# A long convolution and a feed-forward net in one kernel: the first unit's entry rearranged, and a new written-out order

## The chip, the cores and the metric

The kernel runs on one core of a Trainium2 chip. A time is the device time of one execution in microseconds (us). The kernel before took 345.71 us (median of four runs, 345.22 to 345.76). A profile holds one execution, from the core's first instruction to its last; that stretch is its span. The engines of the core work side by side, each through its own queue in order: TensorE (PE, with its weight loads PEld), VectorE (DVE), ScalarE (ACT), GpSimd (POOL), and SyncE (SP), which issues most DMA transfers. They wait for each other by semaphores. Matmul results lie in PSUM and have to be read from there (evicted) by DVE or ACT before the space is used again.

## The reference

Two layers; each adds a gated long convolution and then a feed-forward net to x, which is 2048 rows of 512 columns in bfloat16.

```python
def conv(q, k, v, shift_k, ssm_k, ssm_D):        # all [S=2048, D=512]
    k_shift = sum(pad(k)[t:t + S] * shift_k[:, 3 - t] for t in range(4))
    kv = k_shift * v
    y = irfft(rfft(kv, 2 * S) * rfft(ssm_k.T, 2 * S))[:S]   # causal, per column
    return q * (y + kv * ssm_D)

def ffn(x):                                      # w_gate, w_up: 512 x 1792; w_down: 1792 x 512
    return (silu(x @ w_gate) * (x @ w_up)) @ w_down

for layer in range(2):
    x = x + conv(layernorm(x), k, v, shift_k, ssm_k, ssm_D)
    x = x + ffn(layernorm(x))
```

y does not depend on x, so it is worked out once and used in both layers.

## The kernel before

**Tiling.** The 2048 rows are four blocks of 512. Inside a block row 4p+r lies on partition p as residue r, so a block is a tile of 128 partitions by four rows (r = 0 to 3) by 512 columns. A unit of the feed-forward net is (layer, block, half), two residues, 256 rows. The net (`ffn`) runs over 14 strips of 128 hidden columns: gate and up products of two strips go to a PSUM tile `pf` of 128x512, ACT applies silu to the gate tile (L965) and copies the up tile (L969), DVE multiplies them (L972), and `wd_sb` matmuls (L985) add up in two PSUM tiles `pd`, one for each row. The tile `zT` holds the normalised input with columns on partitions.

**Convolution.** A block's k is turned so that columns lie on partitions, four shifted copies are multiplied by diagonal matrices `dg` of the taps on TensorE, and the sum is multiplied with v on DVE (`shift_mul`, L523 for block 0, L513 and L514 for block 1). Fourier sums by table matmuls (`fwd`) give spectra X of kv and G of the filter, in four slots of a real and an imaginary part. `half` makes G's parts `ev`, which DVE adds and subtracts (`butterfly`, L444 and L446). `product` multiplies X and G on DVE slot by slot (L641, L645) into Z. `inverse_half` forms sums and differences m of Z (L790) and turns them back with table `inv` (L796) into four PSUM tiles, one for each residue; `evacuate_y` (L716) copies tiles to Y on ACT. Later blocks follow while the net runs.

**Entry of the first unit.** `prologue` with `on_pe` multiplies the normalised rows n by y, row 0 straight from PSUM (L902), row 1 from Y (L905), adds them to x (L907), takes the mean and variance (`ln_stats`, L808 to L811, and the power -1/2 on POOL, L813) for both rows together, normalises (L863), turns on TensorE (L919) and copies to `zT` (DVE L922, ACT L924). Other units turn z by DMA (L892). While the entry waits, TensorE works on block 1: its filter's transform, its `shift_mul` and its X.

**Order.** Nothing is left to a scheduler. `Plan.add` records every operation with its engine, an assumed cost, and the buffers that it reads and writes; `Plan.order` takes one list, ORDER, that gives each operation its rank, and lays it in that sequence on its engine's queue. The same walk gives each tile its place in a small ring of buffers: four PSUM tiles `pf`, two `pc`, two `pd`. Costs and `due` times steer the search that made the list and the choice of the ring's place; they execute nothing. In the gaps that the costs foresee before 32 us, `issue` puts filler matmuls (`wm`).

**Around the start.** SP loads h, k, v and x of block 0 and then the weights. Block 0's k is loaded with rows on partitions, turned by TensorE (L365) into PSUM, and copied to `kTb` by `transpose_k` with the four residues interleaved again, two tiles on ACT (L371) and two on DVE (L373). ACT takes the statistics of x's first rows (L827 to L837).

Of the kernel before, what the change touches and what calls it, by code (L numbers as in the profile page):

```python
# [36 lines left out]
KTE = "ADAD"  # L37
# [5 lines left out]
H_SPLIT = False  # L43
PWA = 2.4
# [6 lines left out]
ORDER = [0, 5, 63, 1, 9, 7, 2, 10, 3, 6, 4, 8, 12, 16, 13, 11, 14, 15, 17, 19, 18, 24, 20, 22, 25, 29, 30, 41, 21, 26, 31, 38, 45, 35, 43, 32, 55,  # L51
         42, 51, 64, 74, 59, 71, 100, 104, 70, 76, 23, 27, 28, 37, 53, 39, 65, 44, 36, 34, 50, 58, 69, 72, 47, 40, 33, 46, 56, 62, 48, 61, 49, 60,
         57, 66, 54, 67, 52, 88, 116, 150, 236, 155, 73, 84, 85, 89, 93, 79, 80, 82, 83, 86, 75, 77, 91, 94, 98, 90, 96, 97, 99, 102, 87, 81, 92,
         101, 95, 106, 110, 144, 170, 165, 185, 109, 113, 105, 107, 112, 111, 114, 118, 103, 108, 68, 78, 115, 120, 119, 123, 139, 130, 121, 124,
         127, 125, 129, 132, 140, 142, 148, 134, 138, 141, 154, 158, 161, 136, 146, 152, 117, 122, 128, 126, 133, 137, 143, 145, 160, 147, 173, 178,
         168, 163, 177, 174, 151, 156, 131, 135, 176, 180, 162, 189, 164, 183, 169, 175, 205, 211, 149, 172, 218, 222, 190, 202, 153, 157, 159, 166,
         179, 195, 167, 171, 188, 197, 182, 184, 186, 187, 192, 194, 207, 225, 199, 209, 198, 248, 216, 191, 204, 196, 203, 206, 200, 208, 210, 214,
         215, 219, 226, 230, 237, 224, 228, 233, 231, 241, 246, 256, 249, 258, 262, 275, 274, 280, 277, 283, 287, 291, 296, 292, 298, 299, 302, 309,
         313, 318, 319, 323, 245, 239, 252, 261, 255, 257, 271, 265, 201, 213, 221, 212, 223, 229, 181, 193, 217, 220, 227, 250, 326, 329, 294, 301,
         285, 289, 235, 244, 238, 284, 312, 324, 264, 268, 293, 305, 332, 339, 345, 347, 354, 350, 330, 232, 242, 438, 300, 279, 310, 320, 328, 336,  # L60
         358, 367, 388, 400, 418, 408, 424, 433, 452, 448, 459, 470, 463, 467, 466, 471, 486, 491, 530, 534, 472, 483, 535, 529, 561, 600, 612, 638,
         234, 240, 251, 263, 259, 270, 243, 260, 254, 267, 276, 304, 286, 247, 253, 266, 272, 278, 282, 281, 303, 306, 321, 317, 273, 311, 297, 308,
         290, 295, 269, 288, 315, 327, 333, 314, 322, 307, 316, 325, 331, 335, 334, 338, 343, 359, 352, 361, 340, 351, 337, 344, 362, 368, 370, 348,
         357, 360, 371, 363, 380, 374, 383, 394, 406, 402, 356, 376, 378, 391, 389, 401, 382, 395, 405, 411, 414, 393, 407, 398, 410, 415, 422, 420,
         426, 423, 429, 341, 346, 342, 349, 353, 364, 365, 366, 369, 372, 375, 379, 384, 381, 385, 387, 390, 396, 399, 403, 404, 409, 444, 458, 441,
         456, 462, 464, 474, 476, 478, 484, 489, 497, 492, 499, 503, 505, 517, 526, 514, 518, 436, 447, 446, 451, 428, 445, 425, 430, 481, 510, 494,
         450, 477, 455, 469, 460, 473, 475, 490, 500, 522, 516, 480, 501, 442, 457, 468, 487, 434, 439, 506, 533, 528, 502, 509, 488, 520, 524, 537,
         539, 546, 544, 551, 685, 580, 386, 419, 435, 461, 449, 482, 485, 511, 504, 519, 531, 555, 559, 542, 554, 560, 563, 571, 574, 581, 585, 437,
         496, 397, 413, 498, 513, 540, 527, 545, 548, 578, 589, 590, 593, 604, 607, 631, 667, 616, 618, 377, 373, 412, 355, 432, 421, 443, 427, 532,
         550, 562, 565, 493, 495, 508, 523, 521, 525, 541, 553, 453, 465, 507, 512, 572, 567, 610, 597, 583, 605, 632, 622, 536, 479, 440, 392, 538,  # L70
         591, 602, 599, 629, 623, 416, 595, 431, 454, 515, 614, 626, 635, 640, 658, 662, 651, 645, 690, 694, 720, 723, 697, 703, 727, 730, 698, 701,
         708, 719, 706, 716, 734, 741, 733, 736, 752, 747, 771, 767, 762, 764, 692, 417, 696, 816, 650, 643, 655, 670, 665, 684, 688, 715, 781, 777,
         788, 792, 814, 800, 822, 830, 837, 861, 866, 869, 874, 880, 875, 879, 894, 896, 876, 882, 889, 892, 888, 893, 904, 937, 923, 942, 954, 948,
         961, 966, 973, 984, 1000, 1037, 557, 569, 547, 556, 573, 579, 564, 568, 586, 596, 624, 587, 598, 603, 611, 592, 606, 577, 584, 619, 634,
         639, 543, 549, 570, 575, 552, 558, 566, 576, 594, 637, 659, 601, 609, 582, 588, 617, 646, 666, 649, 669, 677, 680, 683, 630, 647, 648, 654,
         656, 661, 636, 642, 664, 672, 678, 641, 657, 627, 633, 613, 625, 608, 644, 660, 681, 686, 663, 673, 620, 628, 653, 671, 615, 621, 676, 687,
         691, 674, 679, 668, 675, 682, 689, 695, 693, 699, 702, 704, 709, 710, 721, 722, 732, 700, 712, 742, 770, 761, 735, 753, 729, 738, 749, 756,
         717, 726, 759, 786, 779, 744, 750, 754, 768, 740, 748, 758, 763, 773, 790, 783, 774, 780, 766, 784, 787, 793, 796, 797, 801, 804, 705, 711,
         707, 713, 714, 718, 725, 724, 728, 731, 739, 745, 737, 746, 751, 755, 760, 765, 769, 772, 776, 807, 812, 810, 813, 820, 823, 829, 835, 832,
         842, 844, 848, 852, 850, 854, 856, 858, 865, 870, 878, 868, 872, 839, 845, 819, 825, 824, 831, 799, 827, 815, 821, 834, 860, 863, 828, 838,  # L80
         805, 811, 847, 851, 836, 853, 859, 867, 871, 802, 806, 809, 817, 855, 864, 833, 840, 873, 881, 886, 849, 862, 841, 846, 877, 895, 890, 907,
         917, 1054, 946, 743, 778, 782, 789, 785, 791, 795, 826, 883, 900, 908, 915, 918, 911, 919, 922, 925, 936, 938, 941, 940, 950, 885, 891, 898,
         920, 929, 930, 965, 976, 972, 981, 988, 994, 999, 1001, 1003, 1009, 1018, 1021, 1034, 1045, 1036, 1040, 757, 652, 794, 775, 803, 808, 798,
         818, 843, 857, 979, 986, 978, 982, 910, 914, 901, 913, 897, 905, 884, 887, 947, 951, 991, 996, 1004, 1010, 1013, 1007, 1029, 1015, 997,
         1041, 963, 1025, 983, 955, 1061, 969, 1055, 1069, 927, 1052, 1066, 1035, 1022, 1064, 1068, 1085, 1093, 1113, 1098, 1105, 1118, 1142, 1144,
         1148, 1153, 1147, 1151, 1181, 1185, 1168, 1172, 1155, 1158, 1170, 1173, 1174, 1179, 1160, 1162, 1188, 1195, 1199, 1204, 1208, 1202, 1110,
         1058, 1046, 1063, 1107, 1073, 1124, 1145, 1166, 1212, 1215, 1232, 1239, 1247, 1242, 1251, 1255, 1259, 1264, 1268, 1284, 1271, 1274, 1277,
         1281, 1279, 1283, 1293, 1304, 1291, 1299, 899, 903, 902, 909, 924, 931, 906, 921, 934, 944, 949, 935, 945, 928, 933, 939, 952, 912, 926,
         958, 971, 989, 956, 962, 916, 943, 932, 959, 953, 957, 970, 992, 1002, 964, 974, 960, 967, 977, 1024, 1006, 1032, 1031, 1043, 1056, 1050,
         975, 1020, 980, 990, 1012, 1017, 968, 987, 1023, 1042, 1038, 1008, 1014, 998, 1005, 985, 993, 995, 1011, 1027, 1057, 1051, 1026, 1049, 1033,  # L90
         1047, 1019, 1039, 1030, 1044, 1053, 1060, 1065, 1048, 1059, 1016, 1028, 1062, 1070, 1067, 1074, 1072, 1076, 1080, 1089, 1082, 1087, 1077,
         1083, 1075, 1078, 1071, 1088, 1097, 1108, 1129, 1115, 1122, 1112, 1116, 1095, 1126, 1091, 1096, 1128, 1139, 1136, 1086, 1099, 1119, 1132,
         1103, 1109, 1127, 1130, 1135, 1143, 1150, 1133, 1137, 1100, 1106, 1141, 1146, 1154, 1149, 1157, 1079, 1084, 1081, 1090, 1092, 1094, 1102,
         1101, 1104, 1111, 1114, 1120, 1117, 1121, 1123, 1125, 1131, 1134, 1138, 1140, 1152, 1163, 1159, 1164, 1165, 1169, 1178, 1175, 1180, 1184,
         1189, 1193, 1196, 1203, 1197, 1206, 1209, 1219, 1223, 1226, 1229, 1177, 1186, 1156, 1167, 1161, 1176, 1171, 1182, 1192, 1201, 1205, 1211,
         1214, 1194, 1207, 1213, 1218, 1190, 1200, 1222, 1235, 1230, 1198, 1224, 1217, 1221, 1183, 1210, 1187, 1191, 1228, 1238, 1244, 1225, 1234,
# [14 lines left out]
R = 4  # L111
# [126 lines left out]
def kernel(  # L238
# [117 lines left out]
    def transpose_k(b, ring, engs):  # L356
# [3 lines left out]
        for dt in range(KD):  # L360
            pt = new("pc" if dt < 2 else "pd", "pt", [P, R, P], BF16)

            def go(pt=pt, dt=dt):
                for r in range(R):
                    nc.tensor.transpose(pt.t[:, r, :], kn[b].t[:, r, dt * P:(dt + 1) * P], ident.t[:])  # L365
# [921 lines left out]
```

## Time and profile before

| what | us |
|---|---|
| median of four runs | 345.71 |
| the profiled execution's own time | 345.45 |
| its span | 343.7 |
| h of block 0 lands, its turn on TensorE starts | 4.37, 4.41 |
| products X by G start on DVE (L641) | 15.06 |
| second sum m on DVE (L790) | 25.21 |
| row 0 times y (L902) | 26.66 |
| both rows normalised (L863) | 31.38 to 32.12 |
| first feed-forward matmul | 33.46 |

A profile line of a timeline gives start, length, engine, source line, operation, the tile written and those read, shapes, and how many; in brackets stands how long the engine was idle in front of it and what ended that. The lines of a table by stretch give the busy time of each engine with its count of instructions, then TensorE's granted clock as a share (1.00 throughout), the DMA engines' share, and GB/s. Instructions of one engine overlap, so what an instruction costs its engine is the distance between two starts, not its length.

### The profile page before, as it was taken

The page shows a single profiled execution, that of the slowest core. Times are in us where ns is not written, and L with a number is a line of the kernel's source. Part 1 is how long each engine was busy: PE and PEld are TensorE (multiplying, and loading weights), DVE is VectorE, ACT ScalarE, POOL GpSimd, SP SyncE. Part 2 cuts the span into 40 slices and gives each one's busy share as a digit, 9 for nine tenths or more (in the row PEclk, how much of TensorE's full clock was granted, in tenths as well). Part 3 has the DMA queues.
Part 4 walks back from the last instruction along what each step waited for, and adds up shares of the span by engine and source line. Part 5 has one row for each costly group of instructions (what it writes and reads, how often), then busy time and mean ns, then how long its engine had stood idle before and what let it go on. Part 6 is the DMA issues. An engine that isn't in the chain of part 4 may idle for free.

```text
span 343.7 us, 6604 instructions
## 1 busy us (share of the span) xinstructions
PE 338.5 (98%) x2616; PEld 248.1 (72%) x2616; DVE 279.6 (81%) x479; ACT 253.8 (74%) x503; POOL 40.7 (12%) x46
## 2 busy tenths in 40 slices
PE   8999999999999999999999999999999999999996
PEld 6656868777588757778587767767686877777683
DVE  8799999999999997999999999979998524535112
ACT  7899988989788538977699997569774635546362
POOL 4100111102113001212020001111101000100000
PEclk9999999999999999999999999999999999999999
DMA  7999111091110144132101020610202120101101
GB/s 285 312 293 323 43 31 63 15 159 41 34 46 17 31 97 120 23 63 70 32 7 41 2 76 2 127 28 1 32 0 50 26 37 0 24 8 27 41 13 31
DMA packets 42089, 22.96 MB, mean 67 GB/s; under 512 B 33861, under 2 KB 39882, under 8 KB 42058
## 3 DMA queue, kind: packets, MB, share of 16 engines
q1 hardware_dynamic: 41904, 22.47, 26.6%
q8 instruction: 20, 0.33, 0.4%
q14 instruction: 11, 0.09, 0.1%
q10 hardware_dynamic: 154, 0.07, 0.1%
HBM read 12.33 MB, written 2.10 MB: 42 GB/s over the span
## 4 chain that ended last, share of the span: by engine, by line
PE 92%; DVE 3%; DMA 2%; ACT 1%; SPq 0%; issue 0%; ACTq 0%
PE pf L310 57%; PE pd L985 28%; PE ps L310 5%; DMA xc<-in_A_q_dram 2%; DVE t L641 1%; DVE Z L645 1%; PE ps L796 1%; DVE m L790 1%; PE pd L944 1%; ACT jk L833 0%; ACT jk L827 0%; DVE G L444 0%; PE ptz L919 0%; DVE G L446 0%; ACT ev L418 0%
## 5 line engine op out<-in xcount | busy, mean ns | idle before, releaser
L310 PE MATMUL pf<-zT,wg_sb 128*128 128x256 bf16 x896 | 111.0, 273 | 0.0
L310 PE MATMUL pf<-zT,wu_sb 128*128 128x256 bf16 x896 | 110.9, 273 | 0.0
L985 PE MATMUL pd<-wd_sb,ht 128*128 128x512 bf16 (+1 forms) x462 | 105.5, 373 | 0.0
L310 PEld LDWEIGHTS <-wu_sb 128*128 128x128 bf16 x896 | 87.7, 98 | 17.4
L310 PEld LDWEIGHTS <-wg_sb 128*128 128x128 bf16 x896 | 87.7, 98 | 16.3 <-issue 0.3
L965 ACT ACTIVATE sg<-pf 128x512 bf16<-128x512 f32 x112 | 65.4, 604 | 24.4 <-PE pf L310 20.2
L969 ACT CAST ht<-pf 128x512 bf16<-128x512 f32 x112 | 65.0, 594 | 23.5 <-PE pf L310 19.8
L985 PEld LDWEIGHTS <-ht 128*128 128x128 bf16 x462 | 45.2, 98 | 42.8
L972 DVE TENSOR_TENSOR ht<-ht,sg 128x1024 bf16<-128x1024 bf16 (+1 forms) x64 | 39.2, 619 | 24.3 <-ACT ht L969 17.3
L813 POOL TENSOR_TENSOR rstd<-ve,nhalf 128x2 f32<-128x2 f32 x24 | 29.4, 1228 | 204.8 <-DVE ve L811 204.8
L808 DVE BATCH_NORM_STATS2 bnst<-xc 128x6 f32<-128x512 bf16 x48 | 31.5, 685 | 1.9 <-ACT xc L1011 1.3
L1021 ACT CAST dn<-pd 128x512 bf16<-128x512 f32 x24 | 13.5, 594 | 21.5 <-PE pd L985 21.5
L1024 DVE TENSOR_TENSOR xc<-xc,dn 128x1024 bf16<-128x1024 bf16 x12 | 8.3, 689 | 18.7 <-ACT dn L1021 18.5
L652 DVE TENSOR_TENSOR t<-X,G 128x2048 bf16<-128x2048 bf16 x18 | 21.9, 1217 | 0.1
L656 DVE TENSOR_TENSOR t<-X,G 128x2048 bf16<-128x2048 bf16 x18 | 21.9, 1217 | 0.0
L418 ACT ACTIVATE X<-ps 128x512 bf16<-128x512 f32 x32 | 18.9, 611 | 1.0 <-PE ps L457 0.5
L839 POOL TENSOR_TENSOR rstd<-ve,nhalf 128x2 f32<-128x2 f32 x8 | 7.7, 958 | 65.1 <-ACT ve L837 65.1
L418 ACT ACTIVATE H<-ps 128x512 bf16<-128x512 f32 x24 | 13.9, 607 | 1.7 <-PE ps L310 1.5
L664 DVE TENSOR_TENSOR t<-t,t 128x2048 bf16<-128x2048 bf16 x12 | 14.7, 1221 | 0.1
L666 DVE TENSOR_TENSOR Z<-Z,t 128x2048 bf16<-128x2048 bf16 x12 | 14.6, 1220 | 0.1
L310 PE MATMUL ps<-hs,fwd 128*128 128x512 bf16 x40 | 12.5, 379 | 0.3 <-ACT H L418 0.3
L603 ACT ACTIVATE kc<-kTb,tapF 128x512 bf16<-128x512 bf16 x16 | 12.4, 802 | 0.0
(109 smaller groups left out, 325.4 us busy)
## 6 DMA issues: line engine op xcount, KB each, us to landing
hn<-in_A_ssm_k_dram SPq DMA_DIRECT2D x4, 512.0 KB, 6.2
vt<-in_A_v_dram SPq DMA_DIRECT2D x4, 512.0 KB, 6.7
xc<-in_A_q_dram SPq DMA_DIRECT2D x4, 512.0 KB, 4.1
out_dram<-xc SPq DMA_DIRECT2D x15, 128.0 KB, 1.8
wg_sb<-in_B_w_gate_dram SPq DMA_DIRECT2D x1, 1792.0 KB
wu_sb<-in_B_w_up_dram SPq DMA_DIRECT2D x1, 1792.0 KB, 8.2
wd_sb<-in_B_w_down_dram SPq DMA_DIRECT2D x1, 1280.0 KB, 11.5
kn<-in_A_k_dram SPq DMA_DIRECT2D x1, 512.0 KB, 4.4
```

Source lines behind the costliest of these rows:

```text
L310: nc.tensor.matmul(o, lhsT=lhsT, rhs=rhs, start=(n == 0), stop=(n == len(terms) - 1))
L418: add("ACT", act(D), lambda: nc.scalar.activation(out=view(), in_=ps.t[:], func=ACT.Copy, scale=scale), r=[ps], w=[(buf, keys)], conv=conv)
L652: dve(n * D, lambda t1=t1, part=part: nc.vector.tensor_mul(out=t1.t[:], in0=x.t[:, sl, 0, :], in1=g.t[:, sl, part, :]), [(x, key(slots, (0 ...
L656: dve(n * D, lambda t2=t2, part=part: nc.vector.tensor_mul(out=t2.t[:], in0=x.t[:, sl, 1, :], in1=g.t[:, sl, 1 - part, :]), [(x, key(slots ...
L664: dve(n * D, lambda t1=t1, t2=t2, comb=comb: nc.vector.tensor_tensor(out=t1.t[:], in0=t1.t[:], in1=t2.t[:], op=comb), [t2], [t1], conv=conv)
L666: dve(n * D, lambda t1=t1, part=part: nc.vector.tensor_add(out=z.t[:, sl, part, :], in0=z.t[:, sl, part, :], in1=t1.t[:]), [t1], [zk], con ...
L808: add("DVE", 0.6, lambda st=st, i=i: nc.vector.bn_stats(out=st.t[:], in_=xs[c].t[:, i, :]), r=[(xs[c], (i,))], w=[st])
L813: add("POOL", pw, lambda: nc.gpsimd.tensor_tensor(out=rstd.t[:], in0=ve.t[:], in1=nhalf.t[:].to_broadcast((P, n)), op=ALU.pow), r=[ve, nha ...
L965: add("ACT", act(D), lambda ps=ps, o=o, sg=sg: nc.scalar.activation(out=sg.t[:, o:o + 2, :], in_=ps.t[:], func=ACT.Silu), r=[ps], w=[(sg, ...
L969: add("ACT", act(D), lambda ps=ps, o=o, ht=ht: nc.scalar.copy(out=ht.t[:, o:o + 2, :], in_=ps.t[:]), r=[ps], w=[(ht, (o // 2,))], due=(uni ...
L972: dve(n * W, lambda sg=sg, ht=ht: nc.vector.tensor_mul(out=ht.t[:], in0=ht.t[:], in1=sg.t[:]), [sg], [ht], due=(unit, k / pairs, 0.0, "h"))
L985: nc.tensor.matmul((pds[o] if not cs.start else pds[HP]).t[:, cs], lhsT=ht.t[:, q, o * P:(o + 1) * P], rhs=wt["d"].t[:, ft, cs], start=(ft ...
```

## The change

- **Turned k.** `kTb` of block 0 becomes [128, 4 column tiles, 4 residues, 129] with a zero in front of each residue. The four copies out of PSUM are dense, and all on DVE. `shift_mul` reads shifted rows as another residue, dense.
- **Row 1 of the first unit from PSUM.** YD = 2: rows 0 and 1 are multiplied from PSUM; their evictions to Y stay and come after the product.
- **Row by row.** PST: each of the two rows has its own variance and power. FS = 4: of the first two strip pairs, the gate and up tiles are made in two halves of 128 columns, one for each row, so that the first half reads row 0 of `zT` alone.
- **Orders.** ORDER is a new list, of 1577 operations in place of 1571. Read off the two lists, what differs most near the start: the ACT evictions of `ev` parts a and c all come before the statistics of x; one of the G sums (L446) is put before the products with v; ACT's `ve` (L837) comes after the evictions of X's first slot; one product L641 more stands before the first m, and the difference m of the first pair (L790) comes after the second pair's sum; two of block 1's four `shift_mul` rows come before the second pair's inverse; one product L652 for block 1 comes before the second half-unit's L885, not after. SP loads x of block 1 before the second part of `wd_sb`. POOL makes `fq` before the identity. After that the lists hold the same work in other interleavings.
- **Constants.** Assumed costs are changed, and branches are added that the flags leave unused (K_SPLIT, VE_DVE, H1E, "mix", "tapsk").

```diff
-KTE = "ADAD"
+KTE = 'DDDD'
+FS = 4
+PST = True
+YD = 2
...
-        kT[b] = new("k", "kTb", [P, KD, PADL + L], parts=KD + 1)
-        add("POOL", 0.2, lambda: nc.gpsimd.memset(kT[b].t[:, :, 0:PADL], 0.0), w=[(kT[b], (KD,))], due=-48)
+        kT[b] = new("k", "kTb", [P, KD, R, P + 1], parts=KD + 1)
+        add("POOL", 0.2, lambda: nc.gpsimd.memset(kT[b].t[:, :, :, 0:1], 0.0), w=[(kT[b], (KD,))], due=-48)
...
-            dst = lambda dt=dt: kT[b].t[:, dt, PADL:PADL + L].rearrange("d (p r) -> d p r", r=R)
-            src = lambda pt=pt: pt.t[:].rearrange("d r p -> d p r")
+            dst = lambda dt=dt: kT[b].t[:, dt, :, 1:P + 1]
+            src = lambda pt=pt: pt.t[:]
...
+            def at(dt, s):
+                if b:
+                    return kT[b].t[:, dt, PADL + s:PADL + s + R * (P - 1) + 1:R]
+                return kT[b].t[:, dt, s % R, 1 + s // R:1 + s // R + P]
...
-        evacuate_y(k, range(1, R))
+        evacuate_y(k, range(YD, R))
...
-            if i == 0:
-                ps = fresh[c][0]
+            if i in range(YD):
+                ps = fresh[c][i]
...
-                evacuate_y(c, (0,))
+                evacuate_y(c, (i,))
...
-        st = ln_stats(c, rows, 0.85)
+        sts = [ln_stats(c, [i], 0.85) for i in rows] if PST else [ln_stats(c, rows, 0.85)] * HP
...
-            zop = normalise(z, (0,), lambda z=z: z.t[:], c, i, o, st)
+            zop = normalise(z, (0,), lambda z=z: z.t[:], c, i, 0 if PST else o, sts[o])
...
+                    split = unit == (0, 0, 0) and 2 * k + (which == "u") < FS
...
+                    def part(ps=ps, o=o, which=which, fts=fts, i=0):
+                        for q in (0, 1):
+                            ft = fts[o + q]
+                            mm(ps.t[:, q * W + i * P:q * W + (i + 1) * P],
+                               [(wt[which].t[:, kd, ft * P:(ft + 1) * P], zT.t[:, kd, i]) for kd in range(KD)])
...
+                    if split:
+                        for i in range(HP):
+                            add("PE", pe(2 * KD, P), lambda part=part, i=i: part(i=i), r=[(zT, (i,)), wt[which]], w=[(ps, (i,))], due=due)
+                    else:
+                        add("PE", pe(2 * KD, W), go, r=[zT, wt[which]], w=[ps], due=due)
```

## The prediction

> **What bounds the kernel now.** I read the page's first part, then busy time by stage, then TensorE's timeline where the stages show gaps, then VectorE's over the same time. The first lines are the page's busy times and its chain.
>
> ```profile
> PE 338.5 (98%) x2616; PEld 248.1 (72%) x2616; DVE 279.6 (81%) x479; ACT 253.8 (74%) x503; POOL 40.7 (12%) x46
> PE 92%; DVE 3%; DMA 2%; ACT 1%; SPq 0%; issue 0%; ACTq 0%
> ```
>
> TensorE is 92% of the chain. Busy time by stretch (us; length, then PE, PEld, DVE, ACT, POOL, then clock and DMA) says where it is not full:
>
> ```profile
> 4.40:22.00 17.60, 17.41 (x162) 11.25 (x163) 15.74 (x36) 16.01 (x36) 3.63 (x7) 1.00 1.12 302
> 22.00:26.00 4.00, 3.25 (x28) 1.91 (x27) 3.97 (x10) 4.00 (x9) 0.00 (x0) 1.00 1.01 392
> 33.46:46.00 12.54, 12.54 (x106) 10.36 (x106) 12.31 (x19) 11.89 (x29) 1.71 (x2) 1.00 0.19 37
> 46.00:100.00 54.00, 54.00 (x403) 39.15 (x400) 52.71 (x88) 48.28 (x100) 8.14 (x8) 1.00 0.27 55
> 100.00:200.00 100.00, 100.00 (x756) 73.77 (x754) 95.32 (x144) 78.46 (x151) 13.19 (x9) 1.00 0.20 47
> ```
>
> From 33.46 us, where the first feed-forward matmul starts, TensorE has no gap: the end lies a fixed amount of TensorE work behind that point. Only idle time before it can be won, and only by TensorE doing something else in it. TensorE's timeline (start, length, line, shape, count):
>
> ```profile
> 23.10 0.38 PE L796 MATMUL ps<-m,inv 128*128 128x512 bf16 x1
> 23.32 0.28 PE L1253 MATMUL wm<-wz 128*128 128x128 bf16 x2
> 23.89 0.38 PE L310 MATMUL ps<-hs,fwd 128*128 128x512 bf16 x1 [0.30 <-ACT H L418]
> 24.38 0.38 PE L796 MATMUL ps<-m,inv 128*128 128x512 bf16 x1
> 24.59 1.05 PE L310 MATMUL ps<-dg,kTb 128*128 128x128 bf16 x16
> 25.96 0.81 PE L796 MATMUL ps<-m,inv 128*128 128x512 bf16 x3 [0.31 <-DVE m L790]
> 26.61 0.38 PE L310 MATMUL ps<-hs,fwd 128*128 128x512 bf16 x1
> 26.82 1.24 PE L796 MATMUL ps<-m,inv 128*128 128x512 bf16 x5
> 27.90 1.06 PE L310 MATMUL ps<-dg,kTb 128*128 128x128 bf16 x16
> 28.80 0.38 PE L310 MATMUL ps<-hs,fwd 128*128 128x512 bf16 x1
> ```
>
> Matmuls overlap, so pace is read from starts: 5 of width 512 take 26.82 to 27.90, 0.216 each; 16 of width 128 take 27.90 to 28.80, 0.056 each. Idle is a distance between starts less that pace. 24.59 to 25.96 is 1.37 for 0.90 of work: 0.47 idle. 23.89 to 24.38: 0.27. 23.32 to 23.89 holds two fillers only: 0.57. 21.62 to 22.02 in the same view: 0.18. Sum 1.49. The same subtraction where the first unit begins (31.45 to 31.85, the eight transposes from 31.85 to 32.41, 33.06 to 33.46) gives 0.19 + 0.11 + 0.18 = 0.48. So 1.97 us can be won here. Before 22 us TensorE's one other gap (0.34, kn's DMA, before 5.68) stays: the loads keep their order. VectorE is what TensorE waits for at 25.96:
>
> ```profile
> 23.76 1.42 DVE L645 TENSOR_TENSOR Z<-t,t 128x512 bf16<-128x512 bf16 x4
> 25.21 1.29 DVE L790 TENSOR_TENSOR m<-Z 128x1024 bf16<-128x1024 bf16 x2
> 26.66 0.69 DVE L902 TENSOR_TENSOR n<-n,ps 128x512 bf16<-128x512 bf16 x1 [0.15 <-ACT H L418]
> ```
>
> **The change part by part.** VectorE's instructions overlap too; its paces from starts are 0.602 (128x1024 pairs, L641, L790), 0.335 (128x512, L645, L514, L922), 0.67 (a product with a float32 PSUM operand, L523, 10.07 to 10.74 to 11.41).
>
> *Turned k.* Two strided copies on ACT (L371, 0.47 apart) and two on DVE (L373, 0.60 apart: 7.45 to 8.05) become four dense ones on DVE. The nearest dense row is L922, PSUM to SBUF, 0.335: DVE 4 x 0.335 - 2 x 0.60 = +0.14, ACT -0.94. Both lie under TensorE, which is unbroken from 5.68 to 22.0 and gets the same matmuls in another order: nothing by itself. The new copies start at an odd element of rows of 129, which no row here shows; the bounds are 0.335 and the strided 0.60. I take 0.335, since the step is 1 as in L922. At 0.60 DVE carries 1.06 more and the four vt products (L523) end about 0.75 later.
>
> [...]
>
> *Spectrum of block 0.* ACT, relieved, evicts the fourth ev part before the statistics of x (before: 13.25), so one of the two G sums (L446, 0.60) fits in front of the vt products, where DVE sat idle 0.75 (before 10.07), and the other after them. But the product run (L641, 15.06) waits for X0's evictions, not for G. These gain only what ACT puts behind them, the tiny ve (L837, 0.19): start 14.85, 0.21 earlier; bounds 0 and 0.5 (ACT also loses one eviction in front, 0.48).
>
> *The run to the inverse.* From 15.06 to the second sum m at 25.21 is 10.15. The new order takes one difference (L790, 0.602) out of it, behind that sum: 14.85 + 9.55 = 24.40. TensorE, walked along its new order with the paces above: end of block 1's second turn 21.45, first m ready 21.8 (idle 0.3; one product more now lies before it); six spectrum and inverse matmuls (1.30) with 0.1 for the late hs eviction; then two 16-matmul convolutions, moved up from 24.6 and 27.9, fill to 25.0. Their kTb landed at 21.63. Second sum ready 25.15 (idle 0.15), two matmuls, the moved difference 25.75 (idle 0.15). Idle in all 0.7 against 1.49: **-0.79**.
>
> *Row 1 from PSUM, row by row.* The product L902 moves from 26.66 to 26.2. Row 1's product (L905, 0.41) becomes a PSUM one: +0.335 on DVE. In return it waits for two matmuls, not for ACT's eviction (0.60) behind them; that eviction stays, later, on ACT. Row 0 gets its own ve (0.09) and rstd (POOL, two columns took 0.80; POOL idle 15.4 before it). Walk from 26.2: 0.72 product, 0.46 sum, 0.67, 0.61, 0.33, 0.12 aggregate, 0.19 ve, POOL 0.80 from 29.2 to 30.0; DVE meanwhile row 1's statistics and one vt product, to 30.5; z row 0 to 30.9 (before, both rows 31.38 to 32.12). TensorE arrives at 30.7 (31.67 for the same set, less the 0.79 and one matmul moved behind): idle 0.3 instead of 0.48, as row 0's transposes, the two residual adds and row 1's transposes now hide the rest: **-0.18**. Queued behind the added DVE work is conv block 1 (L539 and on), up to 0.4 later.
>
> *Split matmuls.* Four tiles as 16 of width 128 instead of 8 of width 256 (0.108, 40 in 4.37): 4 x (0.90 - 0.87) = **+0.13**.
>
> *Evictions at the start of the unit.* ACT gains nothing there; it is full from 22 to 44.5, and TensorE comes 0.8 to 1 earlier. The fifth to seventh gate and up tiles need PSUM freed by L965 and L969, with two squares (L833, 0.85 each with the accumulator read) interleaved. Bounds 0 and 0.35 on the third; I take 0, the trace having 40 us of those two lines waiting for TensorE and none the other way.
>
> *SP, POOL, costs.* x of block 1 is loaded before the second part of wd (landing 34.34, first used after 46) and so 512 KB earlier, 1.5 us at 347 GB/s: no user nears it. POOL's iota before the identity keeps m4 at 1.6. Cost constants and unused flags run nothing.
>
> Sum: -0.79 - 0.18 + 0.13 = -0.84, from the profiled execution's own 345.45 (span 343.7, 1.75 lies around it and is untouched) to 344.6; from the median 345.71, 0.26 higher, to **344.9**. A kernel like this, whose runs spread over 0.54, can hardly be told from unchanged within 0.2% (0.69 us): 345.02 to 346.40.
>
> **Rivals.**
> - *More than the walk*: all 1.97 goes, less the 0.13: 343.9. For: my walk keeps each wait at its worst. Against: DVE is 99% busy in 22 to 26 (3.97 of 4.00).
> - *Second half-unit late.* In before its second zT transpose is issued at 49.60 and lands 2.4 later, 52.0, against its first use at 53.02: 1.0 of slack. VectorE is full (12.31 of 12.54), carries 0.4 more, and one 1.14 product (L652) now stands in front of L885, its chain: -0.46 + 0.42 + 1.14 = 1.1 later less small gaps, say 0.7. TensorE wants it 0.8 earlier: wait 0.5. Time 345.4. Against: L652 then isn't behind it.
> - *The odd start halves the copies.* vt 0.75 late, of which TensorE's queue hides about half: product run 0.4 later, 345.3.
> - *Slower: an eviction is late in the long part.* The new order of some 1,500 operations must keep 100% from 33 to 340 us. Each time a PSUM tile is freed one ACT instruction late costs its pace, 0.48; two such use up the gain, four give 344.9 + 1.9 = 346.8. For: ACT 48.28 of 54 and DVE 95.32 of 100. Against: no such wait in before.
> - *No effect at all* can't be: four copies change engine and shape.
>
> **How the numbers follow.** Forecast 0.45 (its own range 344.4 to 345.2: the walk's waits put 0.3 to 0.5 either way), more 0.15, half-unit late 0.14, odd start 0.08, late evictions 0.18. Faster (under 345.02): all of the second, four fifths of the forecast, a tenth of the two middle cases: 0.15 + 0.36 + 0.02 = 0.53. Slower (over 346.40): most of the last, 0.16. Same: the rest, 0.31. The range runs from 343.9, the bound of what can be won, to 346.4, where two to three late evictions would put it and about half of the last case is left out.
>
> **What would show it.** Right: the four kTb copies near 0.41 long on DVE; the second m sum near 24.4; TensorE's idle between 21 and 26 near 0.7; the first feed-forward matmul at about 32.2, on 128 columns; no gap after 35. Wrong: kTb copies of 0.68; a TensorE wait for L965 or L969, or at about 52 for zT; X0's evictions not earlier than 15.4.

## The result, and the profile after

The changed kernel takes 346.07 us (median of 45 executions), the kernel before 345.66 (median of 64 beside it): 0.41 us more, a ratio of 1.0016 with a 95% interval of 1.0009 to 1.0022. The forecast was 344.9. The time lies inside the range given and on the other side of no change. Three executions of the experiments below (one of after_fourth, two of after_ht) took 351 us at a lower granted clock (0.993 to 0.995) and are left out of the medians.

The profiled execution of the changed kernel took 347.11 us, its span is 344.5. The page's first part and its chain:

```profile
PE 339.5 (99%) x2646; PEld 249.2 (72%) x2646; DVE 278.6 (81%) x482; ACT 252.8 (73%) x501; POOL 44.0 (13%) x47
PE 92%; DVE 5%; POOL 1%; issue 1%; ACT 0%; POOLq 0%
```

TensorE is as large a part of the chain as before, DVE a larger one. Busy time by stretch (length, then PE, PEld, DVE, ACT, POOL, clock and DMA), with the third stretch again from the first feed-forward matmul, now at 32.88:

```profile
22.00:26.00 4.00, 3.73 (x44) 2.62 (x42) 3.97 (x9) 3.97 (x10) 0.00 (x0) 1.00 0.99 372
32.88:46.00 13.12, 13.12 (x144) 11.32 (x143) 13.02 (x19) 13.09 (x33) 1.57 (x1) 1.00 0.56 127
46.00:100.00 54.00, 53.94 (x399) 38.76 (x398) 51.94 (x88) 48.89 (x100) 9.78 (x8) 1.00 0.17 36
100.00:200.00 100.00, 99.91 (x752) 73.29 (x751) 96.41 (x147) 78.40 (x152) 15.85 (x9) 1.00 0.22 48
```

Between 22 and 26 TensorE is busy 3.73 us instead of 3.25, so the head did what it was to do. But the two last stretches, which were exactly full, have gaps: 53.94 of 54.00 and 99.91 of 100.00.

TensorE's timeline of a second profile of the same kernel (label after_again below), lines that answer to those of before:

```profile
22.00 0.38 PE L819 MATMUL ps<-m,inv 128*128 128x512 bf16 x1 [0.25 <-DVE m L813]
22.21 0.59 PE L317 MATMUL ps<-hs,fwd 128*128 128x512 bf16 x2
22.64 0.38 PE L819 MATMUL ps<-m,inv 128*128 128x512 bf16 x1
23.04 0.59 PE L317 MATMUL ps<-hs,fwd 128*128 128x512 bf16 x2
23.47 1.95 PE L317 MATMUL ps<-dg,kTb 128*128 128x128 bf16 x32
25.26 0.90 PE L819 MATMUL ps<-m,inv 128*128 128x512 bf16 x3
...
32.22 0.39 PE L317 MATMUL ps<-vt,fwd 128*128 128x512 bf16 x1
32.45 1.06 PE L317 MATMUL pf<-zT,wg_sb 128*128 128x128 bf16 x16
```

Two convolutions (32 matmuls, x32) stand where TensorE idled before. Distances between starts less the pace give 0.41 before 22.00, 0.18 before 23.04 and 0.09 inside the three matmuls from 25.26: 0.69 us of idle, against 1.49 before. VectorE at the same place, in the same profile:

```profile
24.43 1.90 DVE L813 TENSOR_TENSOR m<-Z 128x1024 bf16<-128x1024 bf16 x3
26.24 0.68 DVE L929 TENSOR_TENSOR n<-n,ps 128x512 bf16<-128x512 bf16 x1
```

The second sum starts at 24.43 and row 0's product at 26.24, where before had 25.21 and 26.66.

**Where the time went back.** Each profile is cut in three at two marks that both kernels have: the start of the first feed-forward matmul, and the last matmul of all. The clock column is from the clock records of the trace: until that moment matmuls of 128 columns start 0.107 us apart, from then on 0.056. (The clock share of 1.00 in the tables by stretch holds only from there on.)

| kernel, profile | full clock from | first feed-forward matmul | from there to the start of the last matmul | from its end to the end of the span | span |
|---|---|---|---|---|---|
| before | 4.04 | 33.46 | 306.92 | 3.03 | 343.7 |
| before, again | 6.74 | 33.88 | 306.92 | 3.03 | 344.1 |
| changed, the profile above | 6.42 | 32.88 | 307.88 | 3.44 | 344.5 |
| changed, after_again | 4.35 | 32.45 | 307.67 | 3.49 | 343.9 |
| changed, after_third | 4.66 | 32.52 | 307.67 | 3.48 | 343.9 |
| changed, after_fourth | 7.38 | 33.33 | 307.68 | 3.34 | 344.6 |

The first unit begins 1.0 us earlier, and that is lost again in two places: 0.75 in the long part and 0.3 to 0.46 behind the last matmul. (Some 0.4 of the 0.75 is not loss: matmuls that came before the first mark and now follow it, worked out below.) The chip's own contribution, the moment of the full clock, moves either kernel by as much as the whole result: between an early and a late one lie 0.42 us at the first feed-forward matmul of before and 0.88 at that of the changed kernel.

### The profile page after: what moved, and what is told of

It reads as the page before. It is cut to its first block, busy times and chain, and to the rows that moved or that the text cites. A ratio compares the mean times of both kernels' runs of the same rounds, so it can differ in the third digit from the quotient of the medians.

```text
span 344.5 us, 6659 instructions
## 1 busy us (share of the span) xinstructions
PE 339.5 (99%) x2646; PEld 249.2 (72%) x2646; DVE 278.6 (81%) x482; ACT 252.8 (73%) x501; POOL 44.0 (13%) x47
## 4 chain that ended last, share of the span: by engine, by line
PE 92%; DVE 5%; POOL 1%; issue 1%; ACT 0%; POOLq 0%
PE pf L317 53%; PE pd L1024 28%; PE ps L317 7%; POOL rstd L836 1%; PE ps L819 1%; DVE t L664 1%; PE wm L1305 1%; DVE bnst L831 1%; PE pt L494 1%; DVE ht L1011 1%; PE ps L475 1%; PE pd L971 1%; DVE Z L668 0%; DVE m L562 0%; PE pt L379 0%
## 5 line engine op out<-in xcount | busy, mean ns | idle before, releaser
L317 PE MATMUL pf<-zT,wg_sb 128*128 128x256 bf16 (+1 forms) x912 | 110.8, 271 | 0.1
L317 PE MATMUL pf<-zT,wu_sb 128*128 128x256 bf16 (+1 forms) x912 | 109.9, 271 | 0.0
L1008 ACT CAST ht<-pf 128x512 bf16<-128x512 f32 x112 | 63.9, 595 | 21.1 <-PE pf L317 19.3
L836 POOL TENSOR_TENSOR rstd<-ve,nhalf 128x2 f32<-128x2 f32 (+1 forms) x25 | 28.1, 1123 | 206.3 <-DVE ve L834 195.7
L866 POOL TENSOR_TENSOR rstd<-ve,nhalf 128x2 f32<-128x2 f32 x8 | 12.4, 1550 | 61.5 <-ACT ve L864 61.5
L626 ACT ACTIVATE ka<-kTb,tapF 128x512 bf16<-128x512 bf16 x16 | 12.4, 792 | 0.0
```

Source lines behind the costliest of these rows:

```text
L317: nc.tensor.matmul(o, lhsT=lhsT, rhs=rhs, start=(n == 0), stop=(n == len(terms) - 1))
L836: add("POOL", pw, lambda: nc.gpsimd.tensor_tensor(out=rstd.t[:], in0=ve.t[:], in1=nhalf.t[:].to_broadcast((P, n)), op=ALU.pow), r=[ve, nha ...
L1008: add("ACT", act(D), lambda ps=ps, o=o, ht=ht: nc.scalar.copy(out=ht.t[:, o:o + 2, :], in_=ps.t[:]), r=[ps], w=[(ht, (o // 2,))], due=(uni ...
```

## Experiments

Medians are of 9 to 12 executions of each kernel, beside 29 to 34 of the kernel before on the same chip. The same changed kernel lies 0.27, 0.98 and 0.98 above before in three jobs (sets of runs side by side), the same changed head 0.43 below and 0.02 above it: the differences scatter by up to 0.7 us, more than some effects asked for. Only for order_head, head_nosplit, after_third, after_fourth, after_ht and after_ht_act7 does the 95% interval of the ratio to before leave out 1. The profile's own marks are sharper, and verdicts below rest on them where medians don't decide.

| kernel | median us | before, same job | difference |
|---|---|---|---|
| after_again | 346.00 | 345.73 | +0.27 |
| head_after | 345.30 | 345.73 | -0.43 |
| tail_after | 346.46 | 345.73 | +0.73 |
| after_act7 | 345.61 | 345.38 | +0.23 |
| head_act3 | 345.70 | 345.38 | +0.32 |
| order_head | 347.50 | 345.38 | +2.12 |
| head_nosplit | 346.47 | 345.38 | +1.09 |
| after_third | 346.54 | 345.56 | +0.98 |
| after_act7_second | 345.56 | 345.56 | 0.00 |
| head_again | 345.58 | 345.56 | +0.02 |
| head_act7 | 345.44 | 345.56 | -0.12 |
| after_fourth | 346.41 | 345.43 | +0.98 |
| after_ht | 345.96 | 345.43 | +0.53 |
| after_ht_act7 | 346.06 | 345.43 | +0.63 |

The span of every execution is on record too. Pooled over the jobs of the experiments and the result, the medians are 343.8 us for before (124 executions), 344.2 for the changed kernel (79), 343.45 for the changed head (24, head_after and head_again), and 343.7 for the changed kernel with seven copies on ACT (24, after_act7 and after_act7_second).

### Head or long part: the order cut in two

Two kernels take the order apart at its 420th operation, about where the first unit begins. `head_after` has the changed operations:

```diff
-ORDER = [the changed sequence]
+ORDER = [its first 420 operations, then all others in the sequence of before]
```

`tail_after` has the operations of before, their first 420 in the sequence of before and the rest in the changed one. With them went the two kernels themselves.

> The changed kernel once more, to see how much of the profiled execution is its own. Clock theory: the first transposes at 0.107 us a matmul until 6.4 us are a state of TensorE's clock that differs from run to run; in another execution the 0.056 pace can begin near 4.4 us, and the span is then about 0.8 us shorter, near 343.7. Order theory: the late start of the full pace belongs to the change, and comes again near 6.4 us. Either way the waits at 71.3 (0.22) and 145.5 us (0.26) should be there again if they belong to the list of orders. Time: 0.2 to 0.8 us over the kernel before.

> The changed kernel, but only the first 420 operations of its order list (up to the end of the first feed-forward unit); the rest in the order of before. Tail theory (the new order loses about 0.6 us in waits behind 39 us, and the entry wins): no wait near 71 and 145 us, time 345.2 to 345.5, 0.2 to 0.5 under before. Entry theory (the entry itself wins nothing on the chip): time 345.6 to 346.0, not under before. A seam wait of up to 0.5 us near 46 to 55 us would spoil it, and would be seen in the trace.

> The kernel before, with its own entry and the first 420 operations in its own order, and the rest in the order of the changed kernel. Tail theory: slower than before by about 0.5 us (346.1 to 346.3), with the waits near 71 and 145 us. Entry theory: within 0.2 us of before.

> The kernel before once more, for a second trace of its entry. Clock theory: its full matmul pace can begin anywhere between about 4 and 7 us; if it begins late, its span is up to 0.8 us longer than 343.7. Order theory: it begins near 4.0 us as in the first trace, and the span is 343.7 again.

The changed head alone was 0.43 under before, the changed long part alone 0.73 above. The medians point as the tail theory has it, but neither is clear of noise (intervals of the ratio 0.9967 to 1.0013 and 0.9993 to 1.0042). That their sum, +0.30, is near the whole change in the same job (+0.27) is partly chance: neither half has the loss at the end of the kernel that the whole has (below). In the profile of tail_after the stretch from the first feed-forward matmul to the last is 307.40, 0.48 longer than in before, made of TensorE waits of 0.26 at 146.3, 0.07 at 165.1 and 0.15 at 77.3; the rest of the 0.73 stands in no mark of this one profile. The first two stand in every profile of the changed kernel at their place (0.26 to 0.27 near 145, 0.07 near 164), and in none of before or of head_after. A third, for the transposing DMA of `zT`, comes and goes: 0.22 at 71.3 in the first profile of the changed kernel, none in three others, 0.26 at 71.9 in after_act7_second, 0.58 at 71.2 in head_after and none in its repetition. So 0.34 us of loss is fixed in the new order, and a wait that varies from execution to execution comes on top.

The gain of the head is real but smaller than the 1.0 us by which the unit begins earlier. Two later profiles with the changed head and the old order behind it (head_again, head_act7) have 307.33 and 307.34 from the first mark to the last matmul, 0.41 more than before without any wait past 40 us. Of that the split matmuls are 0.13 (sixteen for eight), two small waits at 33.7 and 39.1 make 0.12, and the matmul of `vt` that now follows the first mark is 0.22 by its pace; 0.47, near enough to 0.41.

Before_again (one execution, 345.87 us) has the full clock only from 6.74, and two profiles of the changed kernel show what it does. TensorE's 16 transposes of `hn` and of `kn`, first in after_fourth, then in after_third:

```profile
4.50 1.86 PE L494 MATMUL pt<-ident,hn 128*128 128x128 bf16 x16
6.16 1.64 PE L379 MATMUL pt<-ident,kn 128*128 128x128 bf16 x16
```

```profile
4.50 1.11 PE L494 MATMUL pt<-ident,hn 128*128 128x128 bf16 x16
5.91 1.07 PE L379 MATMUL pt<-ident,kn 128*128 128x128 bf16 x16 [0.30 <-DMA kn<-in_A_k_dram]
```

The same work takes 1.86 and 1.64 us where the full clock came at 7.38, and 1.11 and 1.07 where it came at 4.66. In before a clock 2.7 us later cost 0.42 us at the first feed-forward matmul, because TensorE's wait at 25.96 shrank from 0.48 to 0.12 and took up the rest; in the changed kernel no wait takes it up (0.41 before 22.00 with the early clock, 0.45 with the late one), and 3.0 us later cost 0.88. So the clock theory of the expectations is wrong as an account of the result (the changed kernel is slower at either moment), and yet the clock decides how much the head is worth: 33.46 - 32.45 - 0.41 = 0.60 us with the early clock, 34.10 (tail_after, 7.24) - 33.33 - 0.41 = 0.36 with the late one.

The moments of the seventeen profiles here lie between 4.04 and 7.38, 3.34 apart; what sets them no run shows.

### The end of the kernel: a packet of instructions among the last outputs

From the last matmul's end to the end of the span the changed kernel needs 0.3 to 0.46 us more than before, although the work there is the same. The transfers of the last microseconds of after_again, by queue and by issue (median us from issue to landing):

```profile
q1 hardware_dynamic: 288, 0.20, 10.2%
q10 hardware_dynamic: 144, 0.07, 3.8%
q14 instruction: 1, 0.01, 0.4%
...
out_dram<-xc SPq DMA_DIRECT2D x1, 128.0 KB, 1.7
out_dram<-xc SPq DMA_DIRECT2D x1, 64.0 KB, 2.1
out_dram<-xc ACTq DMA_DIRECT2D x1, 64.0 KB, 2.1
```

One 8 KB packet of an instruction queue (342.1 us in the first profile of the changed kernel, 341.6 here, 336.8 in before) runs beside the outputs, and the two last ones land after 2.1 us. Two theories: the packet holds them up, or the new order's later output of the first row does (its eviction starts 1.28 us before the end of the last matmul in after_again, 2.15 before it in before: 0.87 later, not the 1.25 of the expectation). If the packet's moment depends on how many instructions ACT has run, which was the author's guess, copies on ACT move it; so one-column copies were added there, where ACT waits for TensorE anyway:

```diff
-add("ACT", act(D), lambda ps=ps, o=o, ht=ht: nc.scalar.copy(out=ht.t[:, o:o + 2, :], in_=ps.t[:]),
-    r=[ps], w=[(ht, (o // 2,))], ...)
+def ev(ps=ps, o=o, ht=ht, more=unit == (0, 3, 0) and k < PAD):
+    nc.scalar.copy(out=ht.t[:, o:o + 2, :], in_=ps.t[:])
+    if more:
+        nc.scalar.copy(out=warm1.t[:], in_=nhalf.t[:])
+add("ACT", act(D), ev, r=[ps], w=[(ht, (o // 2,))], ...)
```

with PAD 7 in the changed kernel, 3 and 7 in head_after.

> The changed kernel with seven one-column copies added on ACT in the first half-unit of the last block (about 262 to 282 us), where ACT waits for TensorE; nothing else differs. Code-fetch theory (the 8 KB instruction packet of the second instruction queue, at 342 us in the changed kernel among the packets of the last outputs, at 337 in the kernel before, is set by how many ACT instructions came before it): the packet comes seven ACT instructions earlier, before 338 us; from the end of the last matmul to the end of the span 3.0 us instead of 3.5; 345.6 us, 0.45 under the changed kernel. Late-output theory (the 3.5 come from the order, which puts the last but one eviction 1.25 us later): 3.5 stays, 346.05 us.

> The kernel with the changed head and the old order behind it (345.3 us, instruction packet at 344.0, after the outputs), with three one-column copies added on ACT at the same place. Code-fetch theory: the packet comes three ACT instructions earlier, at about 341 us and so among the last outputs; 3.5 us from the last matmul to the end instead of 3.2 or less; 345.6 to 345.8 us. Late-output theory: no change, 345.3 us.

> The changed kernel once more, beside the next one on the same chip. 3.5 us from the last matmul's end to the end of the span, instruction packet at about 342 us; waits of TensorE of 0.26 near 145 us and 0.07 near 164 us again; 0.2 to 0.45 us above before.

> The changed kernel with the seven one-column copies on ACT once more. Code-fetch theory: 3.0 us behind the last matmul, and 0.45 us under the changed kernel of the same job, so level with before or up to 0.1 under it. Late-output theory: 3.5 us and no difference to the changed kernel.

> Changed head, old order behind it, once more: 0.3 to 0.6 us under before; 3.2 us behind the last matmul; no wait near 145 and 164 us. If the 0.58 us wait for zT at 71 us belongs to this kernel it is there again; if it is the DMA's chance it is another or none.

> The same with seven one-column copies on ACT (three of them cost 0.75 us against before by moving the instruction packet onto the outputs). Code-fetch theory: with seven the packet lies well before the outputs, 3.0 us behind the last matmul; 0.1 to 0.2 us under the kernel without them, 0.4 to 0.7 us under before. Rival (the ACT copies themselves cost time): as slow as with three, 0.3 us above before.

The same window of after_act7_second, the packet now at 326.2:

```profile
q1 hardware_dynamic: 288, 0.20, 8.7%
q10 hardware_dynamic: 144, 0.07, 3.1%
...
out_dram<-xc SPq DMA_DIRECT2D x1, 128.0 KB, 1.7
out_dram<-xc SPq DMA_DIRECT2D x1, 64.0 KB, 1.6
out_dram<-xc ACTq DMA_DIRECT2D x1, 64.0 KB, 1.7
```

| kernel | last packet at | that is, after the last matmul's end | from the last matmul's end to the end |
|---|---|---|---|
| before, tail_after | 336.8, 337.2 | -3.9, -4.6 | 3.03, 3.02 |
| changed (four profiles), after_ht | 341.5 to 342.3, 345.6 | 1.0 to 1.3 | 3.34 to 3.49 |
| changed + 7 copies (two profiles), after_ht_act7 | 324.8, 326.2, 324.9 | -15.4 | 3.02, 3.00, 3.02 |
| changed head (two profiles), head_nosplit | 344.0, 343.4, 345.3 | 3.5 to 3.8 | 3.18, 3.20, 3.19 |
| changed head + 3 | 341.9 | 1.0 | 3.44 |
| changed head + 7 | 336.5 | -3.9 | 3.01 |
| order_head | 345.2 | 2.0 | 3.02 |

Seven copies that do nothing make the end of the changed kernel 0.3 to 0.5 us shorter, three make that of the changed head 0.25 longer, and the order is the same in each pair: it is the packet, not the late output. The late output alone costs nothing: tail_after has it and 3.02, while head_act3 has the early one and 3.44. In every profile the two last outputs are issued 0.27 and 0.44 us behind the last matmul's end; they land after 2.0 to 2.1 us in the six profiles with the packet 1.0 to 1.3 us behind it, and after 1.6 and 1.7 in the eleven others. What the packet doesn't explain is the 3.18 to 3.20 of the kernels where it starts only after the span's end: there the outputs land as early as in before, and the 0.16 more lies behind their landing.

That copies on ACT move the packet is shown by the shift; the packets came much earlier than the seven instructions that were reckoned with (15 us and not 4), so the plain count of these copies does not give the shift, and what does was not shown. The spans of all executions agree with the profiles: 343.7 with seven copies against 344.2 without, a difference of 0.5 with a 95% interval (resampling the executions) of 0.25 to 0.8. The medians of single jobs are too noisy for it: the pair that ran side by side (after_third, after_act7_second) differs by 0.98, twice what the packet explains, the pair after_ht and after_ht_act7 below by 0.10 the other way. head_act7 was expected 0.4 to 0.7 under before and was 0.12 under: not the 0.3 above of its rival, but not shown to be faster than before either (ratio 1.0002, interval 0.9979 to 1.0026), and head_again was level where 0.3 to 0.6 under was expected. (The 0.75 of head_act7's expectation compares head_act3 with head_after, of another job; beside before head_act3 was 0.32 slower.)

### What the head needs: the new operations, and the split

`order_head` is the other half of the question, the operations of before with their first 420 in the changed sequence. `head_nosplit` is head_after with the first four tiles of the unit whole:

```diff
-FS = 4
+FS = 0
```

its whole tiles at the rank that the split tiles' second halves had.

> The operations of the kernel before, their first 420 in the changed order, the rest in the old one. Edits theory (the head's 0.7 us need the new operations: row 1 multiplied from PSUM, statistics row by row, split matmuls, dense copies of k): the waits at 22 to 26 us shrink by the order, but the first unit begins no sooner; first feed-forward matmul under 0.3 us earlier than before, 345.5 us. Order theory (the order alone carries it): first feed-forward matmul 0.6 us or more earlier, 345.1 us.

> The changed head with the old order behind it (345.3 us), the first four tiles of the first unit not split: 32 matmuls of 256 columns in place of 64 of 128. Prediction's view (row 0's transposes, residual adds and row 1's transposes hide the rest; the split costs 0.13): 345.2 us. Rival (the split lets TensorE begin on row 0 while row 1 is still being turned, 0.66 us later): the wait at the first feed-forward matmul grows by about 0.5 and the time is 345.7 us.

The two took 347.50 and 346.47, far slower than either theory said. In order_head TensorE stands still twice:

```profile
32.94 0.40 PE L925 MATMUL ptz<-ident,z 128*128 128x128 bf16 x4 [1.19 <-DVE z L869]
...
35.60 0.38 PE L316 MATMUL ps<-vt,fwd 128*128 128x512 bf16 x1 [1.18 <-ACT X L424]
```

and DVE, whose z is waited for, had itself waited for row 1's eviction and for POOL:

```profile
29.05 0.42 DVE L911 TENSOR_TENSOR n<-n,Yk 128x512 bf16<-128x512 bf16 x1 [0.96 <-ACT Yk L722]
...
32.47 0.41 DVE L869 TENSOR_SCALAR z<-xc,mv,rstd 128x512 bf16<-128x512 bf16 x1 [0.59 <-POOL rstd L819]
```

These account for the first standstill; the second, in front of the `vt` matmul, is the one that whole tiles leave (1.40 by starts in head_nosplit, below, 1.34 here). So the changed head is no better order for the old operations: it needs row 1's product out of PSUM (no eviction to wait for), statistics row by row (row 0 needn't wait for row 1's), and the split tiles. No run takes the first two apart.

The split has a use that the prediction did not see. In head_nosplit, all engines around the first tile:

```profile
32.37 1.22 DVE L567 TENSOR_TENSOR m<-H 128x2048 bf16<-128x2048 bf16 x1
...
33.37 0.70 ACT L441 ACTIVATE X<-ps 128x512 bf16<-128x512 f32 x1
33.51 0.42 DVE L954 COPY zT<-ptz 128x512 bf16<-128x512 bf16 x1
...
34.12 0.38 PE L322 MATMUL ps<-vt,fwd 128*128 128x512 bf16 x1 [1.22 <-ACT X L441]
34.34 0.49 PE L322 MATMUL pf<-zT,wg_sb 128*128 128x256 bf16 x3
```

The new order puts a sum of block 1 (m, 1.22 us) on DVE ahead of row 1's copy to zT, which ends only at 33.93, and ACT frees the PSUM tile of the next `vt` sum only at 34.07. Whole tiles need both rows of zT, so nothing is left for TensorE until then: 1.40 us by starts. Row 0's halves of the first three of the four tiles, 24 matmuls, fill just that time in head_after (32.34 to 33.68; wait 0.05). The rival expected 0.5; the split is worth 1.4 in this order, for 0.13.

### The wait near 145 us

In after_again, VectorE and then TensorE:

```profile
142.87 0.16 DVE L874 SCALAR_TENSOR_TENSOR nmr<-mv,rstd 128x2 f32<-128x2 f32 x1 [0.58 <-POOL rstd L836]
142.95 0.69 DVE L579 TENSOR_TENSOR X<-m 128x1024 bf16<-128x1024 bf16 x1
143.55 1.29 DVE L1011 TENSOR_TENSOR ht<-ht,sg 128x1024 bf16<-128x1024 bf16 x2
```

```profile
143.75 1.04 PE L317 MATMUL pf<-zT,wu_sb 128*128 128x256 bf16 x8
144.90 0.60 PE L1024 MATMUL pd<-wd_sb,ht 128*128 128x512 bf16 x2
```

The down matmul waits for the second gate product, which ends at 144.84, and the sum X (0.60 by its pace) stands ahead of both products. `after_ht` moves it behind them, one operation and nothing else; `after_ht_act7` has the seven copies as well.

> The changed kernel beside the next two on the same chip: 0.26 near 145 us, 0.07 near 164 us, 3.5 us behind the last matmul; 0.3 to 0.6 us above before.

> The changed kernel with one sum of VectorE (X, L579, 0.60 us by its pace, near 143 us) moved behind the two gate products that it stands ahead of. Order theory: no wait near 145 us; from the first feed-forward matmul to the last matmul 307.4 us instead of 307.67, 0.26 us under the changed kernel. Rival (the wait moves on, to the product run behind the sum): another wait of 0.2 to 0.3 between 145 and 165 us and the same time.

> Both cures: that move, and the seven one-column copies on ACT that bring the instruction packet ahead of the outputs. If the wait and the packet are the loss: 0.7 us under the changed kernel, 0.2 to 0.4 us under before; 307.4 us between the first feed-forward and the last matmul, 3.0 us behind it. If something else weighs as much: level with before or above it.

The wait near 145 is gone, and the one near 164 has grown. After_ht_act7, VectorE's and TensorE's timelines:

```profile
142.74 1.30 DVE L1020 TENSOR_TENSOR ht<-ht,sg 128x1024 bf16<-128x1024 bf16 x2
143.95 0.69 DVE L585 TENSOR_TENSOR X<-m 128x1024 bf16<-128x1024 bf16 x1
...
162.86 0.69 DVE L574 TENSOR_TENSOR Z<-m 128x1024 bf16<-128x1024 bf16 x1
```

```profile
163.60 0.59 PE L323 MATMUL ps<-Z,inv 128*128 128x512 bf16 x2 [0.26 <-DVE Z L574]
```

By starts the wait near 164 is 0.42 instead of 0.07, in both kernels; from the first feed-forward matmul to the last after_ht_act7 takes 307.81 against 307.67 (after_ht's 312.15 holds a wait of another kind, see the last section). The sum X was only the place where TensorE noticed that VectorE ran late: give TensorE its 0.26 back and it arrives that much earlier at the next product of the same VectorE. VectorE has nothing to give: from 142.9 to 163.6 us it is never idle for over 0.1 us in after_again or in after_ht_act7, while with the old order (head_again) it still waits 0.26 for POOL at 155.9. (The 0.58 that it waits for POOL in front of 142.87 stands in before too, at 142.27.) The rival of the expectation holds, and the theory that one instruction is to blame falls. What does take both waits away is the old sequence of the whole long part (head_again, head_act7: none). Which of its differences does it stays open. The medians (+0.53 and +0.63) don't tell the two kernels apart; after_ht_act7 stayed above before, not 0.2 to 0.4 under it as expected of the two cures together.

## Why the prediction was wrong

Point by point, against profiles with the early clock (before's, at 4.04, was one):

- *Turned k.* Right. The four copies on DVE start 0.334 apart and last 0.41, at the pace of dense ones, though they begin at an odd element: lines in the section on the hardware. The other bound, the strided 0.60, didn't come.
- *Spectrum of block 0.* Right: the product run starts at 14.79 (after_again), 14.85 forecast, and waits for ACT's X as before.
- *The run to the inverse, -0.79.* Right in mechanism and size: second sum 24.43 (24.40), idle of TensorE 0.69 (0.7).
- *Row 1 from PSUM, row by row, -0.18.* Right: idle 0.13 before row 0's transposes and 0.18 before the `vt` matmul, 0.32 against 0.48. First feed-forward matmul 32.45 (about 32.2); 0.17 of the difference is there before 6 us, where `kn`'s transposes start at 5.85 instead of 5.68. order_head shows that the new order without these edits has a wait of 1.36 in front of row 0's transposes: they were needed, and not only worth 0.18.
- *Split matmuls, +0.13.* The cost was right. What they buy was missed: the step took row 1's zT copy to come without delay, while m stood in front of it on DVE; without the split the head would have lost 1.4.
- *Sum of the head, -0.84.* It came to -0.72 by the waits: 0.69 + 0.32 idle, 0.11 in two new small waits at 33.8 and 39.2, 0.13 for the split, against 1.97. By marks it is 0.60 with the early clock and 0.36 with the late one. The step that added 0.26 to get from the profiled execution to the median treated the clock as a shift that both kernels share. They don't (0.42 against 0.88 us for a clock 3 us later): the idle time that the change removes was what had covered a late clock.
- *"The end lies a fixed amount of TensorE work behind that point."* This step failed, and the sign of the result with it: the stretch did not stay full, and behind the last matmul the time was not fixed either. Two terms that the sum had at nothing: +0.34 for VectorE's late products near 145 and 164 us, and +0.3 to +0.46 for the packet of instructions behind the last matmul. With the head, -0.60 + 0.34 + 0.46 = +0.20 with the early clock (after_again's span less before's: 0.20), -0.36 + 0.34 + 0.31 = +0.29 with the late one; after_fourth less before_again is 0.52, the former's clock 0.64 us later. The median's 0.41 lies between 0.20 and 0.52.
- *The rivals.* The slower one (a late eviction in the long part, 0.48 each, two to use up the gain) had the right place and sign. Its agent was wrong: not ACT freeing PSUM but DVE's gate products and Z, whose 95.32 of 100 us (96.41 in the changed kernel) the prediction listed in the rival's favour without taking DVE for the agent; and it was not two of 0.48 but 0.26 and 0.07. No text before the result had the end of the kernel. The second half-unit's zT did come late in one profile of the changed kernel (0.22 at 71 us), another unit than the one that the rival named.

## What to carry to other kernels

A gain in front of a stretch that is 100% full pays only if that stretch stays full; when a new order comes with it, cut the order at the seam and time both halves before believing either. An idle engine just behind the start may be the cover of a varying clock (here a late one cost 0.42 us with that idle time and 0.88 without): what its removal is worth has to be read from more than one profile. And where the last outputs end the kernel, look for anything else in the DMA queues there, the program's own instructions included; here three or seven added instructions moved that packet from 344.0 us to 341.9 and 336.5.

## What was not expected of the hardware

- **An instruction packet held up the last outputs.** 8 KB in one packet of 0.38 to 0.65 us, and the two 64 KB outputs beside it landed 0.4 us later (2.0 to 2.1 instead of 1.6 to 1.7).
- **The copies to an odd start took no longer than one to an even start.** VectorE in after_again, a dense copy out of PSUM to `hs`, starting at an even bfloat16 element, and the four out of PSUM to `kTb`, each 128x512 and starting at an odd one (of its four rows of 128 two start at an odd element, two at an even one), two to a line:

```profile
6.34 0.41 DVE L512 COPY hs<-pt 128x512 bf16<-128x512 bf16 x1
6.67 0.24 DVE L1182 TENSOR_SCALAR dg<-ident,tapF 128x128 bf16<-128x128 bf16 x1
6.83 0.74 DVE L391 COPY kTb<-pt 128x512 bf16<-128x512 bf16 x2
7.50 0.24 DVE L1182 TENSOR_SCALAR dg<-ident,tapF 128x128 bf16<-128x128 bf16 x1
7.66 0.74 DVE L391 COPY kTb<-pt 128x512 bf16<-128x512 bf16 x2
```

  0.74 for two that overlap is 0.41 for one and 0.33 between starts. The copy to `hs` is 0.41 long too, and the next start lies 0.33 behind its own.
- **One POOL instruction varied by far.** The power for two columns took 1.56 to 1.58 us at this place in every other profile with the changed head and split tiles (1.31 in head_nosplit, 0.96 in before), 5.58 in the profile of after_ht, and ACT waited for it with all its evictions behind:

```profile
37.50 5.58 POOL L871 TENSOR_TENSOR rstd<-ve,nhalf 128x2 f32<-128x2 f32 x1 [6.75 <-ACT ve L869]
```

```profile
43.11 0.48 ACT L883 ACTIVATE nmr<-nm,rstd 128x1 f32<-128x1 f32 x2 [2.77 <-POOL rstd L871]
```

  TensorE then stood still for 2.68 us from 42.8. It ran on at full pace for 0.3 us and then at half pace (matmuls of 256 columns 0.21 apart) until 49.25, with a granted clock of 0.51 (the column behind POOL's):

```profile
45.80:49.30 3.50, 3.50 (x19) 2.51 (x18) 2.92 (x7) 2.51 (x6) 1.03 (x1) 0.51 0.00 0
```

  That execution's span was 348.0. No other profile has this at this place, but the same operation took 4.76 to 4.78 us near 194 us in all nine profiles with the changed long part, and TensorE did not wait there. Eleven executions without a profile, three of them of before, have a mean granted clock of 0.993 to 0.995, as this one has, and spans of 346.8 to 348.7; whether the same instruction was slow in them is not known. What made it slow was not tried.
